# Two plain loads ahead of the transposing ones, setup fills on VectorE, eight sums as two, and new queue orders for every engine

## The chip, the cores and the metric

The kernel runs on one core of one Trainium2 chip. The metric is the device time of one execution in microseconds. TensorE (PE) multiplies, VectorE (DVE) and ScalarE (ACT) do everything between the products, GpSimd (POOL) does small copies and fills, and SyncE (SP) issues most of the transfers. ScalarE issues three small loads as well.

## The reference

`x` is 2 x 16000 x 512 in bf16. A depthwise filter of three taps along time and a SiLU give `z`. Four codebooks of eight vectors quantize it one after another, each on what the earlier ones left. The chosen vectors are summed and filtered by three more taps.

```python
for i in range(K):
    z = z + xp[:, i:i+T, :] * dw_enc[i][None, None, :]
z = _silu(z)
res = z
q = jnp.zeros_like(z)
for s in range(Nq):
    cb = codebooks[s]
    d2 = ...
    idx = d2.argmin(-1)
    sel = cb[idx]
    q = q + sel
    res = res - sel
...
for i in range(K):
    y = y + qp[:, i:i+T, :] * dw_dec[i][None, None, :]
```

## The kernel before

**Tiles.** Time is cut into 18 tiles of up to 16 x 128 = 2048 rows. Tiles 0 and 17 have 6 x 128 rows, tiles 1 and 16 have 8 x 128. Channels lie on the partitions, in four groups of 128 (`KT`), worked on in two halves.

**Loads.** Tiles 0 and 1 (`EARLY = 2`) come by one plain load each (`load_early`, L568) into `STAGE`, which is a part of the last `ZB` buffer, so the profile calls it `ZB`. TensorE transposes them (L579), and VectorE or ScalarE copies the result into `XT` (L589). From tile 2 on, `load` brings each group of 128 rows by a transposing load (L598, with L606 and L612 for the rows before and behind the tile).

**One tile's path.** `front` multiplies by the taps (L639 on ScalarE, L640 on VectorE) and adds (L391) into `ZB`; ScalarE takes an exponential (L645), one of the two adds 1 (L646, L647); `front2` takes a reciprocal (ScalarE, L657) and multiplies it into `ZB` (L391). The two functions of ScalarE need different tables, and each change is an `ACT_TABLE_LOAD`. `select` forms products with the codebooks (L676) and decides three of the four codebooks, one after another, in small VectorE steps. `rows` copies the one-hot rows to `OHR` (L791); `resid` subtracts the chosen vectors on TensorE (L834, L839) and copies the rest back into `ZB` (L861 on ScalarE, L862 on VectorE), decides the fourth codebook (L875 to L891) and copies the windows to `OHW` (L809). `back` forms the output on TensorE (L911 to L915), copies it to `YB` (L920, L921) and stores it (L948). Where TensorE would wait long, the program puts in filler products (L968), whose result is not used.

**Setup.** `setup` builds the constants: transposed codebooks `CBT` and `CBM2` (TensorE L420 and L430, ScalarE copies), the Gram matrix `GP` and its products `BD` (VectorE L391), the decoder rows `WDEC` (TensorE L551, VectorE L553), the selections `DJ`, `SEL`, `SEL3`, the 0/1 column sums `JM` (L496) and `SM` (L524), and fills. `make_identity` on GpSimd gives `IDENT`, which most of it reads. `WENC`, the taps (L397), needs `dw_enc` and the identity. Seven fills are GpSimd's (L381): `MSK`, two `OHD`, `ONES`, `CC2` and two `SEL3` (these lie in an `EX` buffer, so the profile calls them `EX`).

**Order.** The steps are listed by `add` with an engine, a cost and dependencies. The string `RANK` has two characters for each step, in the order of `add`; they are its place in the queue of its engine. The string `WHERE` has one letter for each step that may run on either of two engines (`either`): A for ScalarE, D for VectorE. So the two strings fix what each engine runs in which order; each engine takes its queue in order. The costs only decide which PSUM bank a step gets and where fillers go. There are 2410 steps, 608 of them movable.

Of the kernel before, what the change touches and what calls it, by code (L numbers as in the profile page):

```python
# [185 lines left out]
def kernel(  # L186
# [33 lines left out]
    RANK = ("000102000002060a0M0f0l150i0o0q020a080f0X0n0q0w0p0v0k0s0u0005040B0J010c030k0e0l0h0x090C0t0v0j0K0g0u01090c0f0i0k0n0p070d0e"  # L220
            "0h0j0m0o0q02040b04080a030506010307080d060e0b0g07090h0k0j0i0b090F0I0L0O0S0U130n0E0F0l0H0f0d0h0l10171c0Y1114080g0m0Z121607"
            "050c0s0o000m030n0p0E0G050P0Q0R0T0m0t0j0p040g0r060i0q0u0A0a0z0y0b0z1l1k0w0H020D0e0V0o1g0c0N0d0W1a190r181b1d1e1f0y1s0x1j1h"
            "1i1m1n1o1p0A1v0B1y0D1B0r0s1K1M1N1O1P1Q1R0r0t0L0u1T1V1X1Y1U1W1Z2021220s0v0O0w232426252728292a0t0x0R0y0z2e2f0A0B0T0U0C0D2k"
            "2i0E0F0X0Y0G0H2q2u2x2y2B0K120M150N160X0P1b101q1u1r1t1w0C1x1z0I0Q1A1C0G1D1E1G1F1H0K0M0d060g0c01050407080a0k0l030f0b0j0e09"
            "1L0J1J1I1S0N0P2b0S2l0V2r0W2o0Z2s0I0J2v2A2C2G2H2I2J0v0L140O2L2M2N2P2Q2S2V2W2X2Y0w0Q190R30323435363738390x0S3b0T0U3f1d0V0W"
            "3i1e0X0Y1h3k0Z103m1g11123o3q3u3v3x151m181p1b1u1n191r1a1x1m2h2d2g2c2j2n2m2p102D0r0B0z0i0y0v0w0u0q0t0s0x0n0p0A0o0h0m2w2t2z"
            "112F2K132O181a2R172U2T2Z31333a1c3h1f3n1j3t1l3H13143y16173A3B3D3F3G3I3J0y1c1q1e3L3N3O3S3P3U3V3X3Z410z1i451j434649484a4b4c"
            "4d0D1k1y1l1m1A4o1n1o1C1B1p1q1E1F1r1s1G4u1v1w4G1z1A4N4S4U4Y501J1Q1W231X261Z1Q1Z1T21201P1Y1Y25212127232a261d1f3T1g1h404244"
            "474e4g4i0A1t4w1u4l4n4t4y4x4z4A4B4C4D0B1x1I1y4E4F4H4J4K4L4M4O0C1C1L1D1F1P1R1H1K1T1S1L1M1V1W1N1O1X201U1V5x1Z205z5C5E5I5L27"
            "5R292c282e2s2a2d2b2f2a2r2r2w2t2q2y2v2p2w2k0N0J0P0F0E0D0O0G0R0H0L0M0I0K0T0Q0C0S3d3c3e3g3j1i3l3p1n3K1k3r3s3w3z1o3C3M1t4h15"  # L230
            "0Z1814131711160V1a0U0W1b121c1d190Y3Q3R3W1s3Y1v1w4f1z4q1D4v1H4I1K4X1B1E4V1G1I51535658595c2E5g0F1R5j1S5i5l5n5p5m5r5t5w5D5F"
            "0G2228255H5M5O5K5Q5S5U5W0J2c5Z2f2g2i2h2h2i2j2k2j2m2m2n2n2o2q2o2t2u6t2v2A6F6H6L6R6U2I6Y2T2L2W2N2Q2K2D2N2I2K2O2H2S2K2D2Q2J"
            "2V2T2O4p4m4k4j4r1J4s4P1N541l1i1q1u1v1x1j1k1f1t1p1s1g1e1w1r1h1o4T4Q1M4R4W1O4Z521U5e5a555b575d5h5f5k225y245G295X2b6524265T"
            "2d2e6364676a6d6f3E6h0I2q2p2s6j6l6n6p6k6o6q6r6s6u0L2x6w2z6v6x6y6z6A6B6C6D0P2B2x2D2F6T2A2G2H2B702J2L2E2G2Y312P2Q34357y3739"
            "7J7N7U7W7X3h313l363n38303j343v3d343k353p3a3c3t8c3q3c312k2l692C2E6M6O6P6S6V6X6Z0M2M2F2P7476777975787a7c7d7e0O2X7g2Z7i7j7m"
            "7l7p7q7r7s0Q337v36382W2U3b3d2Z2Y3e3f32303g3i33843o3s8d3u3w8j8m8o8u8A3H8G3Z3A423C3w3V3t3Y3z3A3P3q3U3u3x3N3r3Q3v3F1N1L1O1D"
            "1M1E1F1I1C1K1P1A1H1y1J1z1B1G5s5o5q5u5v5A5B5J2g6g5Y5N5V5P606162662l6m2725291T1U1X28231S1Q1V1Y1R22241W2c0E0H6e6b6c686i2s2u"
            "6E2y7b2z712C722O7x2R2U7f30327t7w7z7A7B7C7E0R3a2V3c7F7G7H7O7L7P7R7T7V7Z0S3m373r8185878e8g8i8l8n0T3x8q3y3z3i3f3A3D3h3j3F3I"
            "3l3o3J3K3p3n3R3T933W3X95979a9e9g433B4f3M4g3Q3H4k3P4p3S3M4i3T4r3W3P4s3V4u3X3W6K6J6I6G6N6Q6W732R7D2m2h2u2p2d2x2j2r2l2b2f2e"
            "2g2o2i2n0K0N2w7h2M7n7k7o7u2S7I2X7Y7M7K7Q7S80828386398p3b8r3e8t3g8I3B3C8w3E3G8C8F8E8H8J8L8M0U3O8Q3S8P8S8U8W8V8Y909194960V"  # L240
            "403x41989b9d9c9f9h9i9j0X449l46473E3F494a9v3J4b4c3H3I4d4e3K3L4h4j9M4n4o9R9T9Xa4a84zag4B414E43464A404C423V4F444G454b4R4f4S"
            "4j4m3L3M8O45489r9w9u9C9E9G9I0W4l3O4m9K9O9Q9U9P9S9Wa3a5a70Y4w3Y4yaaadafacahaiakam114Dao4H4I46474J4K49484L4M4a4b4P4QaM4d4T"
            "4VaT4X4Yb2b6babfbj5a4p5f4u5d4w4A5e4v5m4z4x5l4y5q4B4w5p4A5w4F4J2B2y2J2N2R2C2H2E2v2G2A2z2P2L2I2M2t2F888a898b8f8h8k8s3k8K8y"
            "8v8x8z8B3m8D8N3s992X3b372Y2T3639383d33353a2S2U322W2Z2V8T8X8Z8R923w3y9k3D9y3G9J3N9L3R9Y4q4ta24v4xabajaealaqatau0Z4NaE4Oaw"
            "ayaAaCaHaIaKaLaNaP104UaR4WaQaSaUaVaWaXaYaZ134Z4h5152b84l55564m4n58594o4q5b5c4r4s5g5hbv5k5nbFbJbQbTbV5F4N5J4R5R4U4L5N4S5V"
            "4W4S5S4V5W4X4N5X4Z61514R9n9p9o9m9q9s9t9x3Ua93t3v3h3k3u3i3p3g3q3o3r3l3e3f3m3n3s3j9B9A9z9D9F9H9N9V3Zapa19Za6a0anasarav4caO"
            "4eb04gb44ibq5053bc5457bdbgbiblbnbpbs125ibw5jbubxbBbEbzbCbGbIbKbM145t4D5ubObRbXbWbZc1c3c5155xca5y5z4Hcg5A5B4K4J5C5D4O4M5G"
            "5I4Pco5L5Mcw5P5QcDcIcKcMcO5Z5063536m5h526o5j6r5l4Z6f5g6n5i506e5f6pdK515o5sbS5r5vbYc0c2c4c6c7c8165E4L5Hc9cdcfckcncpcrcscu"
            "cx175Ocz5TcAcCcGcFcNcQcScU186252646555566667585768695a5b6b6d5cdo6g6idw6k6ldGdOdQdSdV6ze06I5w6T5I546P5C6S5G556H5x6M5D536E"
            "5s6G5v563S3G3E3K3B3N3J3z3D3T3R3Q3y3I3C3L3U3OazaDaxaBaFaJaGb14kbtb5b7b3b9bbbhbebk4xbP4e404f473Y483X4c493Z444a4g454143424d"  # L250
            "bm4tbobrbybAbDbH4Ecb4Gci4Icl4QcY5K5UcT5Y60cVcZcXd1d3d5d81a6adb6cdadcdgdidfdhdkdmdndp1b6hdt6jdrdsdudxdAdDdFdH1c6qdJ6t6vdW"
            "5m6w6y5oe16A6C5t5q6D6Fea5u6L6Oep6J6QevexezeBeC6WeJ7c5R7mfy5a7e5S7n5X577g5T7f5V597hfg7l5W584CbLbNbUcccechcj4TcR4o4n4q4i4u"
            "4s4v4r4l4C4t4k4h4y4p4j4B4zcmctcvcqcycBcEcH54d9cLcJcP4YcWd0d2d459dq5edI5kdT5ne76s6udN6x6Be2e5e4e8ebecee1e6K5z6Negeheielen"
            "eoeqeseteu1f6R5E6UeweyeAeDeEeFeGeH1h6XeI6Z70eQ5J72735LeR74765OeX77785Q5P7j7oft7r7wfEfIfSfTg27Ig97S6a7U6b5b7L667P675c7R69"
            "7Zgu5d836f856g5e6V6YeK7175eSeVeTeWeYf0f11g7af57df2f3f4f7fafbfcfdfeff1i7i5U7kfhfjflfkfmfnfofp1l7pfu7s7t5ZfD7v7x61fM7A7D62"
# [80 lines left out]
    JM = [sb([P, 1], F32, f"JM{j}") for j in range(4)]  # L336
# [7 lines left out]
    SM = [sb([P, 1], F32, f"SM{j}") for j in range(SL)]  # L344
# [48 lines left out]
    def setup():  # L393
# [3 lines left out]
        add("DVE", 0.15, ("setup", -7, 0), lambda: nc.vector.tensor_copy(WENC.rearrange("p k i -> p (k i)"), peb()), [], ["WENC"], free=box,  # L397
            after=[len(plan.steps) - 1])
# [12 lines left out]
        for b, t in enumerate(OHD):  # L411
            pool_memset(t, 0.0, [("OHD", b)], 0.6, ("setup", -4, 0))
# [593 lines left out]
```

## Time and profile before

| | us |
|---|---|
| median of 3 runs | 607.35 |
| the runs | 605.89, 607.7, 607.35 |
| profiled execution, its own time | 603.97 |
| its span | 602.2 |

The columns of the queue at the start, from the timeline of the profile: ScalarE's first compute comes at 5.89 us, its first exponential at 20.10, its first change of tables at 25.28. TensorE's granted clock was 0.978 of full speed over the span. The 26 table loads take 1.28 us each. ScalarE holds 114 output copies (L920) and VectorE 12 (L921).

How to read it: busy time is an average over stages with different limits. The page gives the busy time of each engine over the span, and a view by stretch gives the same for each stage. A row of the timeline has start, duration, engine, line, operation, output and input, the count, and in brackets the time that the engine sat idle before it, with what ended this.

### The profile page before, as it was taken

What the parts mean: (1) busy time and instruction counts of PE and PEld (TensorE: products, weight loads), DVE (VectorE), ACT (ScalarE), POOL (GpSimd) and SP (SyncE); (2) the same over time, 40 slices, a digit from 0 to 9 for tenths busy, and PEclk for the clock granted to TensorE, in tenths of its full rate; (3) what the DMA queues carried; (4) which work ended last, traced back from release to release, by engine and by line L of the source; (5) the groups of instructions that cost most, each with busy time, mean ns of one, the idle gap of its engine ahead of it and who ended that gap; (6) DMA issues with size and microseconds to landing.
All of it is one profiled execution on the core that took longest, in us unless ns stands there. A gap on an engine that the chain in (4) does not pass through costs nothing.

```text
span 602.2 us, 27782 instructions
## 1 busy us (share of the span) xinstructions
PE 500.1 (83%) x12621; PEld 240.2 (40%) x12621; DVE 564.9 (94%) x1117; ACT 546.2 (91%) x426; POOL 63.6 (11%) x93
## 2 busy tenths in 40 slices
PE   6979888588878886887787877888797889899995
PEld 3434334343434342343334243343434343445452
DVE  7999999999999999999999999999999999989774
ACT  5889799999999999999999999899999999994553
POOL 2010030000211020001011031101201120000000
PEclk9989999899998999999999988999998999999998
DMA  7534546454455856575875697576674624134146
GB/s 216 95 78 89 99 102 111 73 121 92 67 95 138 188 76 141 108 145 131 168 108 83 145 173 151 143 137 115 125 133 125 118 47 142 40 107 142 37 155 211
DMA packets 155564, 71.84 MB, mean 119 GB/s; under 512 B 146895, under 2 KB 146927, under 8 KB 155318
## 3 DMA queue, kind: packets, MB, share of 16 engines
q1 hardware_dynamic: 155230, 69.64, 53.9%
q8 instruction: 98, 1.61, 1.2%
q10 hardware_dynamic: 216, 0.43, 0.3%
q14 instruction: 20, 0.16, 0.1%
HBM read 2.26 MB, written 32.77 MB: 58 GB/s over the span
## 4 chain that ended last, share of the span: by engine, by line
DVE 35%; ACT 19%; PE 18%; SPq 14%; issue 9%; DMA 4%; POOL 0%; DVEq 0%; ACTq 0%
SPq L598 11%; DVE ZB L391 7%; DVE TA L391 5%; PE banks L834 5%; ACT EX L657 5%; DVE TB L640 5%; PE banks L839 4%; ACT ZB L861 4%; ACT EX L645 4%; DMA XT<-in_x_dram 3%; PE banks L676 3%; DVE TA L640 3%; PE banks L911 2%; ACT YB L920 2%; DVE EX L647 2%
## 5 line engine op out<-in xcount | busy, mean ns | idle before, releaser
L920 ACT CAST YB<-banks 128x1024 bf16<-128x1024 f32 x114 | 111.3, 1032 | 10.9 <-PE banks L911 4.8
L645 ACT ACTIVATE EX<-ZB 128x4096 bf16<-128x4096 bf16 (+2 forms) x36 | 115.5, 3208 | 4.5 <-DVE ZB L391 4.2
L657 ACT ACTIVATE EX<-EX 128x4096 bf16<-128x4096 bf16 (+2 forms) x36 | 115.2, 3202 | 0.1
L861 ACT CAST ZB<-banks 128x1024 bf16<-128x1024 f32 (+2 forms) x108 | 97.6, 955 | 16.0 <-PE banks L839 16.0
L968 PE MATMUL banks<-MSK,IDENT 128*128 128x512 bf16 x402 | 100.2, 390 | 8.2 <-issue 4.2
L676 PE MATMUL banks<-ZB 128*32 128x64 bf16 x8064 | 90.8, 198 | 11.1 <-issue 7.2
L676 PEld LDWEIGHTS <-ZB 128*32 128x32 bf16 x8064 | 76.3, 96 | 57.2 <-issue 50.1
L748 POOL COPY OHD<-OHA 128x256 bf16<-128x256 bf16 (+2 forms) x36 | 45.6, 1267 | 408.2 <-DVE OHA L391 377.6
L911 PE MATMUL banks<-WDEC,OHW 128*128 128x512 bf16 x252 | 74.6, 389 | 10.5 <-ACT YB L920 3.7
L839 PE MATMUL banks<-OHR,WR 32*128 32x512 bf16 (+2 forms) x1152 | 81.3, 353 | 0.6 <-issue 0.6
L640 DVE TENSOR_SCALAR TB<-XT,WENC 128x2048 bf16<-128x2048 bf16 (+2 forms) x119 | 80.2, 685 | 0.9 <-DVE EX L647 0.6
L391 DVE TENSOR_TENSOR TA<-TA,TB 128x4096 bf16<-128x4096 bf16 (+2 forms) x36 | 72.6, 2017 | 0.5
L391 DVE TENSOR_TENSOR ZB<-TA,TB 128x4096 bf16<-128x4096 bf16 (+2 forms) x36 | 72.6, 2018 | 0.4 <-ACT TB L639 0.2
L391 DVE TENSOR_TENSOR ZB<-ZB,EX 128x4096 bf16<-128x4096 bf16 (+2 forms) x36 | 72.4, 2015 | 0.4 <-ACT EX L657 0.4
L834 PE MATMUL banks<-ZB,IDENT 64*64 64x512 bf16 (+2 forms) x576 | 55.6, 365 | 14.3 <-ACT ZB L861 4.8
L968 PEld LDWEIGHTS <-IDENT 128*128 128x128 bf16 x402 | 37.9, 100 | 53.0 <-issue 16.7
L834 PE MATMUL banks<-ZB,UP 64*64 64x512 bf16 (+2 forms) x576 | 52.8, 350 | 0.0
L639 ACT ACTIVATE TB<-XT,WENC 128x2048 bf16<-128x2048 bf16 (+2 forms) x25 | 44.5, 1785 | 2.6 <-DVE TA L391 2.0
L839 PEld LDWEIGHTS <-WR 32*128 32x128 bf16 x1152 | 23.2, 92 | 58.7 <-issue 50.3
L640 DVE TENSOR_SCALAR TA<-XT,WENC 128x2048 bf16<-128x2048 bf16 (+2 forms) x64 | 43.2, 681 | 0.7 <-DMA XT<-in_x_dram 0.4
L834 PE MATMUL banks<-ZB,DOWN 64*64 64x512 bf16 (+2 forms) x576 | 41.2, 361 | 0.0
L862 DVE CAST ZB<-banks 128x1024 bf16<-128x1024 f32 (+2 forms) x36 | 34.4, 959 | 5.6 <-PE banks L839 5.4
(133 smaller groups left out, 580.8 us busy)
## 6 DMA issues: line engine op xcount, KB each, us to landing
out_dram<-YB SPq DMA_DIRECT2D x33, 448.0 KB
out_dram<-YB SPq DMA_DIRECT2D x28, 512.0 KB
XT<-in_x_dram SPq DMA_TRANSPOSE x267
out_dram<-YB SPq DMA_DIRECT2D x30, 60.0 KB
ZB<-in_x_dram SPq DMA_DIRECT2D x1, 1024.0 KB
ZB<-in_x_dram SPq DMA_DIRECT2D x1, 768.0 KB
out_dram<-YB SPq DMA_DIRECT2D x31, 2.0 KB
out_dram<-YB SPq DMA_DIRECT2D x2, 224.0 KB
```

What stands on the lines that cost most here:

```text
L391: add("DVE", cost, key, lambda: nc.vector.tensor_tensor(out=out, in0=a, in1=b, op=op), reads, writes, **kw)
L598: nc.sync.dma_start_transpose(out=X[:, :, g + 1, :], in_=src[g])
L640: lambda dst=dst, src=src, w=w: nc.vector.tensor_scalar(out=dst, in0=src, scalar1=w, scalar2=None, op0=ALU.mult),
L645: add("ACT", act(2 * R), ("exp", n, h), lambda: nc.scalar.activation(v(ex), Z, ACT.Exp, scale=-1.0), zt, [("EX", sl), "ACTTAB"], hold="E")
L657: nc.scalar.add_instruction(mybir.InstActivation(name=nc.get_next_instruction_name(), engine=mybir.EngineType.Activation, func=ACT.Reciprocal,
L676: nc.tensor.matmul(o[HB * q:HB * (q + 1), u * ZW:(u + 1) * ZW].rearrange("p (s c) -> p s c", s=2), lhsT=blk, rhs=both, start=False, stop=( ...
L834: nc.tensor.matmul(at(r)[to], lhsT=dia[h, h], rhs=Z[h, i, r:G:RG, :], start=start, stop=False)
L839: nc.tensor.matmul(at(r), lhsT=WR[v][g, i * P:(i + 1) * P], rhs=W[g, v // 3, 0:rows_of[r], :], start=False, stop=stop)
L861: either({"ACT": act_psum(2 * k * P), "DVE": dve(2 * k * P)}, key(1), lambda dst=dst, src=src: nc.scalar.copy(dst, src()), lambda dst=dst, ...
L911: nc.tensor.matmul(o, lhsT=W[:, k, PADC:PADC + P], rhs=WDEC[u], start=True, stop=not wrap)
L920: either({"ACT": act_psum(1024), "DVE": dve(1024)}, key, lambda dst=dst, box=box: nc.scalar.copy(dst, ps(box)), lambda dst=dst, box=box: n ...
L968: nc.tensor.matmul(PS[j // 2][:, 512 * (j % 2):512 * (j % 2) + NMK * ZW], lhsT=IDENT, rhs=MSK.rearrange("p u w -> p (u w)"), start=True, s ...
```

## The change

Five things are done:

1. The two plain loads of tiles 0 and 1 are the first two entries of SP's queue. The transposing loads of tile 2 list them as predecessors (`after=first_loads`). The planner's guess of how long a plain load takes changes.
2. Seven fills move from GpSimd to VectorE: `MSK` (128 x 512), two `OHD` (128 x 1024), `ONES` (128 x 128), `CC2` (24 columns of f32) and two `SEL3` (32 x 256); bf16 except `CC2`.
3. The four sums into `JM` become one into a tile `JMT` with four columns, and the four into `SM` one into `SMT`.
4. `RANK` and `WHERE` are new strings, for 2404 steps.
5. With them many movable steps change engine: of the taps with 2048 rows 8 go from VectorE to ScalarE and 4 back; of the output copies 8 and 7; of the corrections' copies with 1024 columns 10 and 9; of the copies to `OT` 4 and 12.

The heads of the queues, read off the strings:

| queue | before | after |
|---|---|---|
| SP | load 0, one transposing load, load 1, transposing loads | load 0, load 1, transposing loads |
| ACT | three loads, then codebook copies | two loads, one `CBM2` copy, the load of `WDBC`, codebook copies |
| PE | codebook, `ROW` product, Gram product, tile 0's first group, `WDEC` products, tile 1's first group, ... | codebook, tile 0's three groups, one group of tile 1, Gram product, ... |
| DVE | one `JM` sum, a fill, `DJ`, a fill, `SM`, `WENC`, ... | 17 fills, some copies and the two sums, `WENC` as the 25th, ... |

```diff
-        pool_memset(MSK, 0.0, ["MSK"], 0.8, ("setup", -6, 0))
+        dve_memset(MSK, 0.0, ["MSK"], 0.3, ("setup", -6, 0))
...
-            pool_memset(t, 0.0, [("OHD", b)], 0.6, ("setup", -4, 0))
+            dve_memset(t, 0.0, [("OHD", b)], 0.45, ("setup", -4, 0))
...
-        pool_memset(ONES, 1.0, ["ONES"], 0.3, ("setup", -5, 0))
+        dve_memset(ONES, 1.0, ["ONES"], 0.15, ("setup", -5, 0))
...
-        pool_memset(CC2, 0.0, ["CC2"], 0.2, ("setup", -5, 0))
+        dve_memset(CC2, 0.0, ["CC2"], 0.1, ("setup", -5, 0))
...
-        idv = IDENT.rearrange("p (s j c) -> p s j c", s=Nq, c=C)
-        for jj in range(4):
-            add("DVE", 0.2, key, lambda jj=jj: nc.vector.tensor_reduce(out=JM[jj], in_=idv[:, :, jj, :], axis=AX.XY, op=ALU.add), ["I"],
-                [("JM", jj)])
+        idv = IDENT.rearrange("p (s j c) -> p j s c", s=Nq, c=C)
+        add("DVE", 0.25, key, lambda: nc.vector.tensor_reduce(out=JMT, in_=idv, axis=AX.XY, op=ALU.add), ["I"], [("JM", jj) for jj in range(4)])
...
-            pool_memset(t, 0.0, [("SEL3", a), ("EX", NE - 1)], 0.4, ("setup", -5, 0))
+            dve_memset(t, 0.0, [("SEL3", a), ("EX", NE - 1)], 0.2, ("setup", -5, 0))
...
-        add("SP", 0.6, ("load", n, 0), lambda: nc.sync.dma_start(out=rows, in_=src), [], [("STAGE", n)], tail=2.0 + 0.35 * G)
+        first_loads.append(add("SP", 0.6, ("load", n, 0), lambda: nc.sync.dma_start(out=rows, in_=src), [], [("STAGE", n)], tail=2.4 + 0.3 * G))
...
-            add("SP", 1.4, ("load", n, 0.01 * g), lambda g=g: one(g), [], [("X", st["xb"], g + 1)], tail=1.5)
+            add("SP", 1.4, ("load", n, 0.01 * g), lambda g=g: one(g), [], [("X", st["xb"], g + 1)], tail=1.5, after=first_loads if n == EARLY else ())
```

The sums into `SM` change as those into `JM`.

More of the change, by code (lines that the diff above doesn't have):

```diff
@@ L343 @@
     WR = [sb([P, D], BF16, f"WR{v}") for v in range(4)]
-    SM = [sb([P, 1], F32, f"SM{j}") for j in range(SL)]
+    SMT = sb([P, SL], F32, "SMT")
+    SM = [SMT[:, j:j + 1] for j in range(SL)]
     MV = [sb([P, 1], F32, f"MV{v}") for v in range(3)]
@@ L605, in load @@
             before = xf[r0 - 1:r0 - 1 + G * P, :].rearrange("(p g) d -> g p d", g=G)[0]
-            add("SP", 1.4, ("load", n, 0.01 * G), lambda: nc.sync.dma_start_transpose(out=X[:, :, 0, :], in_=before), [], xe, tail=1.5)
+            add("SP", 1.4, ("load", n, 0.01 * G), lambda: nc.sync.dma_start_transpose(out=X[:, :, 0, :], in_=before), [], xe, tail=1.5, after=first_loads if n == EARLY else ())
         else:
```

105 lines of the change are left out of this document (53 added, 52 removed).

## The prediction

> **What bounds the kernel now.** I read the page first, then busy time by stretch, then VectorE's timeline where the last stretch begins.
>
> ```profile
> span 602.2 us, 27782 instructions
> ...
> PE 500.1 (83%) x12621; PEld 240.2 (40%) x12621; DVE 564.9 (94%) x1117; ACT 546.2 (91%) x426; POOL 63.6 (11%) x93
> ```
>
> Two engines are almost full, and TensorE's 83% contains fillers. Which engine is last depends on the stage. The columns below are the stretch, its length, and busy time with instruction counts of PE, PEld, DVE, ACT and POOL, then the granted clock and the DMA share.
>
> ```profile
> 0.00:46.00 46.00, 36.39 (x301) 18.00 (x301) 40.04 (x136) 35.84 (x52) 6.40 (x34) 0.96 0.54 129
> 46.00:523.60 477.60, 393.41 (x10326) 188.27 (x10330) 467.23 (x832) 463.26 (x322) 54.37 (x49) 0.98 0.59 117
> 523.60:590.00 66.40, 65.10 (x1894) 31.55 (x1884) 52.49 (x142) 43.26 (x50) 2.84 (x10) 1.00 0.32 111
> 590.00:602.20 12.20, 5.21 (x125) 2.42 (x124) 5.16 (x10) 3.87 (x4) 0.00 (x0) 0.87 0.63 202
> ```
>
> Up to 523.6 us VectorE is busy 507.3 us, so it idles 6.0 us in the head and 10.4 us in the body. From 523.6 to 590 TensorE is busy 65.1 of 66.4 us: that stretch is TensorE's, and the last 12.2 us are one chain. The border is this copy of tile 14's one-hot rows, with the wait before it in brackets:
>
> ```profile
> 522.78 0.29 DVE L391 TENSOR_TENSOR OHD<-KEY,M 128x128 bf16<-128x128 f32 x1
> 523.57 0.69 DVE L791 COPY OHR<-banks 128x1024 bf16<-128x1024 bf16 x1 [0.49 <-PE banks L786]
> ```
>
> TensorE's corrections of tile 14 (L841) wait for it. In the old and the new rank string TensorE has the same steps behind that point (100 of 533), and the final steps stand in the same order. So the time is the moment at which VectorE reaches this copy, plus 78.6 us that hardly shrink: TensorE idles 1.3 us before 590. The moment is VectorE's work ahead of the copy plus its idle time ahead of it. ScalarE is busy 499.1 us up to there and idles 24.5, so it is not the last.
>
> **The head now.** Start, duration, engine, line, tile, and the idle time before:
>
> ```profile
> 0.74 0.40 SPq L568 DMA_DIRECT2D ZB<-in_x_dram  x1
> ...
> 1.20 1.29 SPq L598 DMA_TRANSPOSE XT<-in_x_dram  x1
> ...
> 1.34 0.18 DVE L496 TENSOR_REDUCE JM<-IDENT 128x1 f32<-128x32 bf16 x1 [1.34 <-POOL IDENT masks.py:199]
> ...
> 1.80 0.43 ACTq L376 DMA_DIRECT2D YB<-in_dw_dec_dram  x1
> ...
> 2.55 0.56 SPq L568 DMA_DIRECT2D ZB<-in_x_dram  x1
> ...
> 4.11 0.17 DVE L397 CAST WENC<-banks 128x12 f32<-128x12 bf16 x1 [1.71 <-PE banks L396]
> ...
> 5.66 0.28 PE L420 MATMUL banks<-IDENT,CB 32*128 32x32 bf16 x4 [1.58 <-DMA CB<-in_codebooks_dram]
> ...
> 6.29 0.44 PE L430 MATMUL banks<-IDENT,CB 32*64 32x32 bf16 x6
> ...
> 6.88 1.03 PE L579 MATMUL banks<-IDENT,ZB 128*128 128x128 bf16 x8
> ...
> 10.36 1.04 PE L579 MATMUL banks<-IDENT,ZB 128*128 128x128 bf16 x8
> ...
> 13.98 0.69 DVE L589 COPY XT<-banks 128x1024 bf16<-128x1024 bf16 x1 [0.35 <-PE banks L579]
> ...
> 14.99 0.41 DVE L640 TENSOR_SCALAR TB<-XT,WENC 128x768 bf16<-128x768 bf16 x1
> ...
> 20.10 1.52 ACT L645 ACTIVATE EX<-ZB 128x1536 bf16<-128x1536 bf16 x1
> ...
> 28.09 0.96 DVE L391 TENSOR_TENSOR ZB<-ZB,EX 128x1536 bf16<-128x1536 bf16 x1
> ```
>
> VectorE starts at 1.34 us, when the identity is there, and waits another 1.71 us. Tile 0's transposes (L579) run from 6.88 us, between codebook work, and its taps start at 14.99 us.
>
> **The change, part by part.**
>
> **Plain loads first.** One transposing load is no longer between them, so the second is issued at about 1.2 us instead of 2.55. Its rows were used at 10.36 us and will be there about a transposing load (1.29 us) earlier, or more. The transposing loads of tile 2 move back by one plain issue, 0.4 us of a queue whose work is wanted only after the first two tiles; I take nothing. ScalarE's queue now issues the load of `WDBC` behind its first `CBM2` copy, which waits for the codebook: from 1.80 to about 6.1 us. TensorE wants it behind tile 0's and tile 1's transposes, near 11 us. It was used at the latest 6.2 us after issue (by 8.0), so TensorE could wait up to 1.3 us; its cover is the transposes, and I take nothing.
>
> **Memsets on VectorE.** Seven cross over. Rows for their price, and for the fused sums (tile and shape, count | busy, mean ns of one):
>
> ```profile
> L381 POOL MEMSET OHD<- 128x1024 bf16 x1 | 1.0, 1035 | 0.0
> ...
> L388 DVE MEMSET OHA<- 128x16 uint32 x8 | 0.5, 72 | 0.0
> ...
> L388 DVE MEMSET OHW<- 128x8 uint32 x6 | 0.4, 65 | 0.0
> ```
> ```profile
> L524 DVE TENSOR_REDUCE SM<-IDENT 128x1 f32<-128x32 bf16 x4 | 1.2, 288 | 0.0
> L496 DVE TENSOR_REDUCE JM<-IDENT 128x1 f32<-128x32 bf16 x4 | 0.7, 167 | 1.3 <-POOL IDENT masks.py:199 1.3
> ...
> L469 DVE TENSOR_REDUCE GD<-IDENT 128x16 f32<-128x128 bf16 x1 | 0.3, 254 | 0.0
> ```
>
> The two DVE rows give 7 ns for 8 more words: 0.9 ns a word on a base of 58 ns. A bf16 zero fill goes out as 32-bit words here (`OHA` is bf16 in the kernel), so 1024 elements are 512 words: 0.5 us for each `OHD`, 0.3 for `MSK`, 0.17 each for `ONES` and the two `SEL3`, 0.08 for `CC2`: 1.9 us. Without that packing it is twice the slope, about 3.4 us. I take 1.9, because both rows show packed words. The Trainium skill, page "VectorE: DVE Perf Modes", section "Zero memsets can be issued as uint32 (trn2)", says that a memset costs one cycle an element whatever the type, so only packing of zeros halves it; the trace's rows have that form, and by the page `ONES`, a fill with 1.0, stays unpacked, which these sums already have. The fills stand first in VectorE's new queue, before 4.11 us, where it idles 1.34 + 1.71 us now. If that cover went, 1.9 us would move the end.
>
> **Eight sums as two.** They take 1.2 + 0.7 us, or about 1.4 without overlap (neighbouring VectorE instructions overlap by some 0.07 us); the two new ones cost about 0.3 each by the L469 row. That is -0.8 us, with bounds of 0 and -1.4.
>
> **The head with all of it.** TensorE starts on the codebook at 5.66 us as now. Ten small transposes (0.28 + 0.44 us for ten) stand ahead of tile 0's three groups (about 1.0 each), so these end near 9.3, the copies near 10, and taps start at 10 instead of 14.99. VectorE's steps up to tile 0's first `ZB` add up to 5.2 us, so the first exponential comes at 15.3 instead of 20.10. But the products that used to fill the waiting (nine `BD`, four `WDEC`) now stand behind it, and the same addition puts the first gate product at 29.4, against 28.09. VectorE's idle time in the head falls from 6.0 to 3.8 us: 0.7 at the start, about 2 around tile 0's transposes, 1.1 in tile 0's decisions. That is **-2.2 us**. Its work ahead of tile 0's corrections grows by **2.4**: 0.8 in the setup (fills 1.9, less the fused sums and two `WR` products that change engines, less small reorderings), 1.3 for two `XT` copies taken from ScalarE, the rest in small ones.
>
> **All queues anew.** The strings fix each engine's order and the engine of every movable step, so I counted what VectorE has ahead of the copy at 523.57 in each, at these rows less the overlap:
>
> ```profile
> L640 DVE TENSOR_SCALAR TB<-XT,WENC 128x2048 bf16<-128x2048 bf16 x93 | 69.1, 751 | 0.8 <-DVE EX L647 0.6
> ...
> L862 DVE CAST ZB<-banks 128x1024 bf16<-128x1024 f32 x20 | 24.3, 1217 | 1.9 <-PE banks L839 1.9
> L921 DVE CAST YB<-banks 128x1024 bf16<-128x1024 f32 x12 | 14.5, 1219 | 2.7 <-PE banks L911 2.1 <-issue 0.4
> ...
> L758 DVE COPY OT<-banks 128x128 bf16<-128x128 bf16 x13 | 2.8, 217 | 0.4 <-PE banks L753 0.4
> ```
>
> Behind the head: four taps fewer (-2.7), taps of tiles 16 and 17 brought ahead (+2.0), two output casts (+2.3), six copies to `OT` (+0.9), one window copy (+0.6), corrections (-0.5): **+2.6 us**. ScalarE's own count changes by +0.7, and its table switches stay at 25. Whether the 2.6 cost anything depends on where they lie: in VectorE's 10.4 us of idle body they cost nothing, outside them 2.6.
>
> **Sum.** Head +2.4 - 2.2 = +0.2. Body: 2.6 us go into holes (0), and of the other 7.8 us of holes I take a third as closed, -2.6, between none and all, since the orders of all engines are new and no row shows the new waits. Together -2.4 us. On the profiled execution's 603.97 us (span 602.2) that is 601.6; the three runs lie at 605.89 to 607.7, all above it, and against their median of 607.35 it is **604.95**.
>
> **The rivals.**
>
> *Work brought ahead pushes the border (slower).* Place: VectorE ahead of the copy at 523.57. The added 2.6 us fall where it is already busy, and no hole closes: +0.2 + 2.6 = +2.8, so 610.15; with half of them in holes it is 608.85. It decides once VectorE idles more than 11.3 us before that copy (16.3 now, less the 5.0 us of added work). For it: VectorE is busy 467.2 of 477.6 us in the body, so little room is left. Against: a third of the holes is enough to hide the 2.6.
>
> *Most holes close (much faster).* Two thirds of the 7.8 us go: +0.2 - 5.2 = -5.0, so 602.35. For it: the order is what makes these waits. Against: tile 14's decisions wait on other engines in any order, as the 0.49 us at the copy shows.
>
> *The codebook lands behind the second plain load.* Up to 4.2 us, and from there to 5.05 (queue, packets, MB, share; q1 is SP's, q10 ScalarE's):
>
> ```profile
> q1 hardware_dynamic: 102, 0.63, 46.4%
> q10 hardware_dynamic: 24, 0.00, 0.4%
> ```
> ```profile
> q1 hardware_dynamic: 321, 0.23, 84.6%
> q10 hardware_dynamic: 51, 0.04, 20.7%
> ```
>
> The codebook's 0.03 MB, issued at 1.42, moved only when the first plain load's 0.79 MB were nearly through. Now 1.05 MB more stand right behind on SP's queue. If the codebook waits for these too, at the 322 GB/s of that stretch or the some 400 of a full one, it lands 2.5 to 3.2 us later, and TensorE holds tile 0's transposes behind it: -2.4 + 2.5 = +0.1, so 607.45. Against: ScalarE's queue got its turn when the load ahead of it was done. The Trainium skill, "DMA: Bandwidth & Descriptors", section "Queues, rings and completion order", has each DMA engine change between queues after a whole packet; by that rule the codebook comes between the two plain loads and lands as now, and the rows above agree so far.
>
> **How the numbers follow.** Forecast 0.50 (own range 603 to 607), border pushed 0.22, most holes close 0.14, codebook late 0.14. Less than 0.3% (1.8 us) cannot be told from no change here. Faster: 0.41 of the forecast, 0.14, and 0.04 of the late codebook, 0.59. Slower: 0.18 of the pushed border, 0.02 of the late codebook, 0.01 of the forecast, 0.21. Same: 0.20. The range 600.5 to 610.5 takes in the lower half of closing holes and the pushed border, and leaves out the case in which both the fills cost 3.4 us and no hole closes.
>
> **What would show it.** Right: L568 twice before any L598; VectorE's fills before 4 us with the 1.71 us gone; L640 from about 10 us; the first L645 near 15.3; the L391 gate near 29; L791 of tile 14 near 521 with VectorE's idle time ahead of it near 8.9 us; 78 us from there to the end. Wrong: L420 past 7 us (codebook late), fills longer than 0.8 us each, VectorE idle over 11 us ahead of that copy, or a stretch behind it that differs by more than 2 us, which would break the argument that it is TensorE's.

## The result and the profile after

| comparison | kernel before, median | changed kernel, median | ratio, 95% interval |
|---|---|---|---|
| first (12 and 12 runs) | 607.53 us | 603.06 us | 0.9934, 0.9910 to 0.9958 |
| second (29 and 12 runs) | 606.09 us | 603.55 us | 0.9948, 0.9927 to 0.9969 |

The change made the kernel faster by 0.5 to 0.7%; the medians lie 4.5 and 2.5 us apart, and 604.95 was forecast. Among the 29 runs of the kernel before in the second comparison, a granted clock lower by 0.01 goes with some 1.8 us more; the changed kernel's runs had 0.977 on average there and those 0.975, so by estimate some 0.4 us of the 2.5 may be the clock's. The two profiled executions of the prediction's pair lie only 1.5 us apart (span 602.2 and 600.7), because that of the kernel before was faster than all twelve unprofiled runs beside it (604.66 to 609.39). So a trace on each side isn't enough here, and both kernels were traced a second time.

The page of the changed kernel, its first lines:

```profile
span 600.7 us, 27780 instructions
...
PE 500.1 (83%) x12632; PEld 241.1 (40%) x12632; DVE 562.4 (94%) x1125; ACT 548.7 (91%) x419; POOL 53.6 (9%) x86
```

Busy time by stretch, cut at the new moment of tile 14's copy (columns as in the prediction: PE, PEld, DVE, ACT, POOL), and the copy itself:

```profile
0.00:46.00 46.00, 31.64 (x272) 16.19 (x273) 40.16 (x133) 33.74 (x50) 2.55 (x28) 0.93 0.56 131
46.00:523.23 477.23, 398.00 (x10367) 190.54 (x10369) 469.24 (x846) 465.85 (x316) 47.58 (x48) 0.99 0.60 116
523.23:590.00 66.77, 65.90 (x1983) 32.74 (x1976) 48.97 (x139) 44.32 (x51) 3.48 (x10) 1.00 0.37 127
590.00:600.70 10.70, 4.54 (x56) 1.67 (x40) 4.04 (x9) 4.80 (x5) 0.00 (x0) 0.87 0.54 175
```
```profile
523.23 0.68 DVE L792 COPY OHR<-banks 128x1024 bf16<-128x1024 bf16 x1
```

VectorE has 509.4 us of work ahead of the copy (507.2 before, up to that copy's start) and idles 13.8 us (16.3 before). TensorE is busy 65.9 of the 66.8 us behind it, as before, and the copy now waits for nothing. The head of the changed kernel, from its timeline:

```profile
0.74 0.91 SPq L569 DMA_DIRECT2D ZB<-in_x_dram  x2
...
0.86 0.27 DVE L390 MEMSET MSK<- 128x256 uint32 x1 [0.86 <-PEq L991]
1.19 0.48 DVE L390 MEMSET OHD<- 128x512 uint32 x1
...
1.81 0.17 DVE L390 MEMSET ONES<- 128x128 bf16 x1
...
7.00 0.23 PE L432 MATMUL banks<-IDENT,CB 32*64 32x32 bf16 x2 [3.44 <-DMA CB<-in_codebooks_dram]
...
9.00 0.69 DVE L590 COPY XT<-banks 128x1024 bf16<-128x1024 bf16 x1 [2.89 <-PE banks L580]
...
11.58 0.42 DVE L641 TENSOR_SCALAR TA<-XT,WENC 128x768 bf16<-128x768 bf16 x1
...
16.63 1.48 ACT L646 ACTIVATE EX<-ZB 128x1536 bf16<-128x1536 bf16 x1 [0.39 <-DVE ZB L393]
...
29.95 0.95 DVE L393 TENSOR_TENSOR ZB<-ZB,EX 128x1536 bf16<-128x1536 bf16 x1
```

The fills stand where they were expected, at the prices expected. But TensorE starts on the codebooks at 7.00 us instead of 5.66, and VectorE waits 2.89 us behind that. Three views of the DMA queues, up to 4.2 us, from there to 5.05 (q10 moves nothing) and from 5.05 to 6.3 us, show the codebooks' 0.03 MB on q10 in the last, which in the prediction's trace of the kernel before had moved by 5.05:

```profile
q1 hardware_dynamic: 121, 0.73, 45.0%
q10 hardware_dynamic: 24, 0.00, 0.4%
```
```profile
q1 hardware_dynamic: 56, 0.33, 93.1%
```
```profile
q1 hardware_dynamic: 64, 0.52, 100.1%
q10 hardware_dynamic: 42, 0.03, 7.9%
```

### The profile page after: what moved, and what is told of

Same layout as the page of the kernel before. It is cut to its first block, busy times and chain, and to the rows that moved or that the text cites. A ratio compares the mean times of both kernels' runs of the same rounds, so it can differ in the third digit from the quotient of the medians.

```text
span 600.7 us, 27780 instructions
## 1 busy us (share of the span) xinstructions
PE 500.1 (83%) x12632; PEld 241.1 (40%) x12632; DVE 562.4 (94%) x1125; ACT 548.7 (91%) x419; POOL 53.6 (9%) x86
## 4 chain that ended last, share of the span: by engine, by line
DVE 23%; PE 12%; SPq 8%; ACT 8%; issue 5%; DMA 1%; DVEq 0%; ACTq 0%
SPq L599 7%; DVE ZB L393 6%; DVE TB L641 3%; PE banks L835 3%; PE banks L912 3%; PE banks L677 2%; PE banks L840 2%; DVE TA L393 2%; ACT ZB L862 2%; DVE TA L641 2%; ACT EX L646 2%; DVE EX L648 1%; ACT YB L921 1%; DVE ZB L863 1%; DMA XT<-in_x_dram 1%
## 5 line engine op out<-in xcount | busy, mean ns | idle before, releaser
L862 ACT CAST ZB<-banks 128x1024 bf16<-128x1024 f32 (+2 forms) x109 | 97.7, 952 | 16.3 <-PE banks L840 16.3
L969 PE MATMUL banks<-MSK,IDENT 128*128 128x512 bf16 x413 | 103.5, 392 | 6.4 <-issue 2.6
L912 PE MATMUL banks<-WDEC,OHW 128*128 128x512 bf16 x252 | 74.0, 382 | 14.3 <-ACT ZB L862 8.0
L641 DVE TENSOR_SCALAR TB<-XT,WENC 128x2048 bf16<-128x2048 bf16 (+2 forms) x115 | 76.7, 676 | 1.6 <-issue 1.2
L835 PE MATMUL banks<-ZB,IDENT 64*64 64x512 bf16 (+2 forms) x576 | 54.3, 368 | 13.4 <-DVE ZB L863 3.0
L749 POOL COPY OHD<-OHA 128x256 bf16<-128x256 bf16 (+2 forms) x36 | 27.5, 764 | 417.3 <-DVE OHA L393 417.3
L969 PEld LDWEIGHTS <-IDENT 128*128 128x128 bf16 x413 | 38.4, 100 | 49.7 <-issue 13.8
L640 ACT ACTIVATE TB<-XT,WENC 128x2048 bf16<-128x2048 bf16 (+2 forms) x29 | 53.2, 1845 | 3.6 <-DVE TA L393 2.0
L863 DVE CAST ZB<-banks 128x1024 bf16<-128x1024 f32 (+2 forms) x35 | 32.8, 950 | 7.3 <-PE banks L840 7.3
```

The lines of the kernel that those rows point to most:

```text
L640: either({"ACT": act(R), "DVE": dve(R, 3.84) + 0.06}, key, lambda dst=dst, src=src, w=w: nc.scalar.mul(dst, src, w), lambda dst=dst, src=s ...
L641: lambda dst=dst, src=src, w=w: nc.vector.tensor_scalar(out=dst, in0=src, scalar1=w, scalar2=None, op0=ALU.mult),
L835: nc.tensor.matmul(at(r)[to], lhsT=dia[h, h], rhs=Z[h, i, r:G:RG, :], start=start, stop=False)
L862: either({"ACT": act_psum(2 * k * P), "DVE": dve(2 * k * P)}, key(1), lambda dst=dst, src=src: nc.scalar.copy(dst, src()), lambda dst=dst, ...
L912: nc.tensor.matmul(o, lhsT=W[:, k, PADC:PADC + P], rhs=WDEC[u], start=True, stop=not wrap)
L969: nc.tensor.matmul(PS[j // 2][:, 512 * (j % 2):512 * (j % 2) + NMK * ZW], lhsT=IDENT, rhs=MSK.rearrange("p u w -> p (u w)"), start=True, s ...
```

## The experiments

The moment of tile 14's copy, the rest behind it (span less moment), and VectorE's busy and idle time ahead of it were read the same way in every trace, from the copy's row and the view by stretch:

| profiled execution | its time | moment | rest | VectorE busy | idle |
|---|---|---|---|---|---|
| before | 603.97 | 523.57 | 78.6 | 507.2 | 16.3 |
| before, second trace | 608.32 | 528.45 | 78.0 | 507.9 | 20.6 |
| changed | 602.52 | 523.23 | 77.5 | 509.4 | 13.8 |
| changed, second trace | 603.50 | 524.01 | 77.7 | 509.4 | 14.6 |
| edits on the old order | 609.10 | 528.50 | 78.8 | 508.2 | 20.3 |
| the same, second trace | 608.74 | 528.17 | 78.7 | 507.7 | 20.5 |
| the same, fills on GpSimd | 607.59 | 527.65 | 78.2 | 507.1 | 20.5 |
| new order alone | 608.94 | 528.89 | 78.1 | 511.4 | 17.5 |
| the same, second trace | 606.57 | 525.75 | 79.1 | 511.1 | 14.7 |
| changed, fills on GpSimd | 602.22 | 522.75 | 77.6 | 510.4 | 12.4 |
| changed, codebooks first | 603.59 | 523.88 | 77.8 | 509.8 | 14.1 |
| changed, stores on GpSimd | 602.97 | 523.01 | 78.2 | 509.8 | 13.2 |
| changed, work added early | 611.10 | 531.51 | 77.8 | 515.0 | 16.6 |
| changed, work added late | 609.82 | 530.24 | 77.8 | 514.9 | 15.4 |

**Both kernels once more.** No edit.

> The kernel before, unchanged, for a second trace and as a null comparison. Expected: a ratio within 0.3% of 1. The first profiled execution took 603.97 us while twelve unprofiled ones took 604.66 to 609.39. If the end is set by the moment of VectorE's one-hot copy of tile 14 plus a tail of TensorE, a slower profiled execution must show the extra time as VectorE's idle time ahead of that copy (more than 16.3 us) or as a tail longer than 78.6 us, with busy times as before. If both stretches keep their length relative to the span, a lower clock made all instructions longer.

> The changed kernel, unchanged, for a second trace and a second comparison. Expected: 603 us and a ratio of 0.9934 within 0.25%. In its trace TensorE's tail behind tile 14's copy should be 77 to 79 us, as in the six traces so far, and whatever differs from the first trace should be VectorE's idle time ahead of the copy.

Before: 607.71 us, ratio 1.0014 (0.9994 to 1.0035). Changed: the second row of the first table. The slower execution of the kernel before has its 4.4 us as VectorE's idle time (20.6 against 16.3 us), with busy time and rest almost as before (0.6 us more and 0.7 less): the first possibility named. Some 3.0 us of the 4.3 are one wait, at a tap for a transposing load; the longest such wait in the first trace is 0.4 us. From the timeline of the second trace:

```profile
417.57 0.75 DVE L640 TENSOR_SCALAR TA<-XT,WENC 128x2048 bf16<-128x2048 bf16 x1 [3.41 <-DMA XT<-in_x_dram]
```

Against this execution the change is worth 4.4 us at the copy: 1.6 us more work and 6.0 us less idle time. Two stretches of the second traces show where, before and then changed (0 to 203 us, and 397 to 471):

```profile
0.00:203.00 203.00, 163.53 (x3131) 80.14 (x3132) 191.50 (x385) 183.56 (x144) 21.86 (x48) 0.97 0.54 107
...
397.00:471.00 74.00, 60.52 (x1803) 29.89 (x1802) 69.90 (x125) 69.42 (x48) 7.19 (x6) 0.95 0.63 122
```
```profile
0.00:203.00 203.00, 163.28 (x3246) 81.72 (x3280) 195.18 (x392) 188.07 (x143) 17.79 (x44) 0.97 0.54 108
...
397.00:471.00 74.00, 61.11 (x1746) 30.27 (x1752) 71.58 (x128) 70.43 (x52) 7.35 (x6) 0.98 0.62 118
```

In the first 203 us VectorE does 3.7 us more (195.18 against 191.50) in the same time, and ScalarE 4.5 more; from 397 to 471 us VectorE does 1.7 more, where the old order had its long wait. The other stretches up to 524 us differ by 0.3 us or less. The first traces don't repeat this: up to 203 us VectorE does only 0.4 us more there (192.80 against 192.37), and the rest of the difference is spread over the later stretches. So where the gain arises differs from execution to execution.

**The edits on the old order**, twice, and once with the fills left on GpSimd.

In short (the strings are left out):

```diff
 RANK, WHERE: those of before, but
-SP:  load 0, transposing load, load 1, ...
+SP:  load 0, load 1, transposing load, ...
-DVE: JM sum, fill, DJ, ... (eight sums); GpSimd: seven fills
+DVE: six fills, ... (two sums), one SEL3 fill once its place is free
```

> The three edits alone (both plain loads at the head of SP's queue, the seven fills on VectorE, eight mask sums as two) on the old order and the old choice of engines. Theory A, the gain comes from the new order of the body: the head's waits shrink by some 2 us, the fills cost as much, the time is 0 to 1.5 us below the kernel before (606 to 607.5). Theory B, the gain is in the head edits: at least 3 us below (604.5 or less). Theory C, the fills are paid in full: 1 to 2 us above.

> The three edits on the old order once more, for a second trace at an ordinary time, since the first profiled execution was one of the slowest of its kernel (609.1 against a median of 605.5). If the edits alone are worth 1.7 us, the ratio is again 0.995 to 0.999; its trace should then show VectorE past the head no later than in the kernel before and fewer or shorter waits for transposing loads. If the first ratio was chance, it is 1 within 0.3%.

> The old order with both plain loads at the head of SP's queue and two mask sums instead of eight; the seven fills stay on GpSimd. In the run with all three edits on the old order VectorE waited 3.0 us in the head for TensorE, which waited for the codebooks. Theory: the late codebooks cover the fills, so the fills cost nothing there, and this kernel takes what the three edits took together (605.5) within 0.3%, with tile 0's first gate at the same 29.1 us. Rival: the fills are paid, and this kernel is 1.9 us below it (603.6) with the gate near 27.3 us.

Ratios 0.9972 (0.9947 to 0.9996), 1.0024 (0.9999 to 1.0050) and, without the fills, 1.0015 (0.9992 to 1.0039). The first alone would have said 1.7 us faster; the repetition said the opposite. The two intervals just miss each other, so they are too narrow for comparisons made on different chips, and a single ratio nearer to 1 than about 0.3% is not to be read. Together they show no gain. Both traces with all three edits agree: 20.3 and 20.5 us idle, as in the second trace of before, and the first gate no earlier (29.15 and 29.23 us; 28.09 and 28.98 before). The head's waits of the first of them:

```profile
DVE GR L449 <- PE banks L445: 3.0, 1, 3.0
DVE rr L709 <- PE banks L675: 1.0, 1, 1.0
DVE MSK L390 <- PEq L989: 0.9, 1, 0.9
DVE WDEC L552 <- PE banks L550: 0.5, 1, 0.5
```

The 1.71 us of waiting for `WENC`'s product are gone (0.4 in the second trace), and 3.0 us (2.5) at the Gram matrix, which needs the codebooks, are new. With the fills on GpSimd the gate comes at 29.14 us, so the fills cost nothing here that shows, as expected: the wait for the codebooks covers them.

**The new order alone**, twice: the strings of the change, with the transposing load between the plain loads, the fills on GpSimd and eight sums.

In short again:

```diff
 RANK, WHERE: those of the change, but
-SP:  load 0, load 1, transposing load, ...
+SP:  load 0, transposing load, load 1, ...
-DVE: seven fills, two sums
+DVE: eight sums; GpSimd: seven fills
```

> The new order and the new choice of engines alone: one transposing load is between the two plain loads again, the seven fills are on GpSimd, eight mask sums instead of two. Theory A: most of the gain of the whole change stays, 2.5 to 4.5 us below the kernel before (603 to 605). Theory B: no gain (607.5 within 0.3%), since without the edits the new order has nothing to draw on. By the addition of VectorE's work, 2.6 us more stand ahead of tile 14's copy than before; if no wait closes, it is 2 to 3 us slower than before (609.5 to 610.5).

> The new order without the edits once more, for a second trace and comparison (the first profiled execution was the slowest of its kernel, 608.9 against a median of 605.3). If the order is worth 2 us alone, the ratio is again 0.995 to 0.9997. Its work on VectorE ahead of tile 14's copy is more than before; the gain must show as idle time of VectorE in the body, below the 10.4 to 14.3 us of the old order.

Ratios 0.9974 (0.9950 to 0.9997) and 0.9976 (0.9951 to 1.0001): about 1.5 us of the gain. Each ratio is too near to 1 to be read alone; that two chips agree speaks for it. It is less than theory A asked and more than theory B. What was expected of the second trace is not seen: VectorE's idle time in the body (from 46 us to the copy) is 13.5 and 11.5 us in these two traces, and not below the old order's range of 10.4 to 14.3. What is less is the head's, 3.9 and 3.2 us against 6.0 and 6.3. Both profiled executions were slower than the median of their twelve, by 3.7 and 2.4 us. Here the first codebook product starts at 5.59 us in both traces, against 6.91 to 7.07 in the nine with both plain loads ahead and the codebooks on ScalarE's queue: the late codebooks come from the loads. The head is none the worse for the missing edits (first gate at 29.42 and 28.54 us; 29.95 with them), so what the whole change has beyond the order isn't in the head. One place shows in the traces: from the copy of tile 12's one-hot rows to that of tile 13's it takes 29.87 and 29.60 us here, and 28.0 us in all seven other traces on the new order. First the second trace of the new order alone, then the second trace of the changed kernel:

```profile
468.91 0.60 PE L968 MATMUL banks<-MSK,IDENT 128*128 128x512 bf16 x2
...
470.58 0.82 PE L968 MATMUL banks<-MSK,IDENT 128*128 128x512 bf16 x3 [1.06 <-issue]
471.24 0.38 PE L911 MATMUL banks<-WDEC,OHW 128*128 128x512 bf16 x1
...
472.13 1.01 ACT L920 CAST YB<-banks 128x1024 bf16<-128x1024 f32 x1 [1.47 <-issue]
...
480.99 0.23 DVE L758 COPY OT<-banks 128x128 bf16<-128x128 bf16 x1 [1.19 <-PE banks L753]
```
```profile
469.05 0.82 PE L912 MATMUL banks<-WDEC,OHW 128*128 128x512 bf16 x2 [0.27 <-DVE OHW L810]
...
470.34 1.03 ACT L921 CAST YB<-banks 128x1024 bf16<-128x1024 f32 x1
470.36 0.81 PE L969 MATMUL banks<-MSK,IDENT 128*128 128x512 bf16 x3 [0.49 <-issue]
...
479.54 0.21 DVE L759 COPY OT<-banks 128x128 bf16<-128x128 bf16 x1
```

The order of the steps is the same. But five fillers stand ahead of tile 11's output products in the first and three behind them in the second: the planner places fillers by the steps' costs, and undoing the edits changes these. TensorE comes to the products 2.2 us later, ScalarE waits 1.47 us for its cast, its casts of the rest come late, TensorE's corrections wait for those, and VectorE waits 1.19 us for a transpose queued behind them. Between 430 us and tile 14's copy this trace loses 1.5 us on the changed kernel's second trace and 1.3 on its first, nearly all of it at this place. The medians on one chip put what the edits add in all at 1.1 us (604.14 against 603.06 with the fills on GpSimd, below) and at 1.9 us (605.27 against 603.42 with the codebooks first). So probably most of it is a side effect of their costs. The run with the codebooks first has the PSUM banks of the new order alone in tile 12's corrections and no such wait, so it isn't the banks; no run moves the fillers alone, so this cause is argued from the rows and not shown by a run.

**The changed kernel with its fills back on GpSimd** (4 of the planner's 433 bank choices differ, none behind the setup).

```diff
-        dve_memset(MSK, 0.0, ["MSK"], 0.3, ("setup", -6, 0))
+        pool_memset(MSK, 0.0, ["MSK"], 0.8, ("setup", -6, 0))
...
```

> The changed kernel with the seven fills back on GpSimd; loads first, two sums and the new order stay. Extra work on VectorE behind the head went to the end in full (7.55 us of fills made the kernel 7.0 and 7.9 us slower). Theory: in the head the wait for the codebooks covers the fills, so tile 0's first gate stays at 29.9 us and the time at that of the changed kernel, 603.3 within 0.3%. Rival: the fills are in VectorE's way in the head too, the gate comes 1 to 2 us earlier and the time falls as much. Third: GpSimd is late with them, and it is slower.

603.06 us, ratio 0.9964 (0.9935 to 0.9993, which takes in the changed kernel's two ratios); the first gate at 29.89 us. The theory holds as far as this can tell: where the fills run makes no difference that shows. The rows of the head show something else, told in the last section.

**The codebooks first.**

```diff
-    jw = add("ACT", 0.6, ("setup", -9, 0), lambda: nc.scalar.dma_start(out=CB1, ...), writes=["CB1"], tail=2.2, after=[jw])
+    jw = add("SP", 0.4, ("setup", -9, 0), lambda: nc.sync.dma_start(out=CB1, ...), writes=["CB1"], tail=2.2)
```

> The changed kernel with one move: the load of the codebooks goes from ScalarE's queue to the head of SP's queue, ahead of both plain loads. In the changed kernel TensorE waits for it until 7.00 us and VectorE idles 2.89 us behind that. If VectorE's idle time in the head goes straight to the border (theory A of the prediction: moment of the copy is work plus idle), the time is 1.5 to 2.5 us below the changed kernel, 600.5 to 601.5. Rival: a later wait in the body takes up what the head gives back, and the time stays at that of the changed kernel, 603 within 0.3%. If the plain loads come later by as much, tile 0's first transposes wait for these instead and the gain is under 1 us.

603.42 us in six runs, ratio 0.9931 (0.9906 to 0.9956): the changed kernel's time. The head did gain: first codebook product at 2.95 us, first gate at 27.74 instead of 29.95. Theory A misses: tile 14's copy comes at 523.88 us, between the changed kernel's 523.23 and 524.01, so none of the 2.2 us shows at the border. The rival says that later waits take them, and these are VectorE's longest at taps:

```profile
114.69 0.75 DVE L641 TENSOR_SCALAR TA<-XT,WENC 128x2048 bf16<-128x2048 bf16 x1 [0.95 <-DMA XT<-in_x_dram]
...
179.38 0.75 DVE L641 TENSOR_SCALAR TB<-XT,WENC 128x2048 bf16<-128x2048 bf16 x1 [1.35 <-issue]
...
213.72 0.75 DVE L641 TENSOR_SCALAR TA<-XT,WENC 128x2048 bf16<-128x2048 bf16 x1 [1.44 <-issue]
```

The first is a wait for a transposing load; the two with "issue" have no releaser in the profile, but stand at the same kind of step. VectorE's steps have the same order in these kernels, so the same taps can be compared. In the changed kernel's second trace they start at 115.33, 179.15 and 211.97 us, with no wait over 0.5 us: the lead of 2.2 us is gone at the second. In its first trace they start at 116.99, 181.56 and 214.37 us:

```profile
116.99 0.75 DVE L641 TENSOR_SCALAR TA<-XT,WENC 128x2048 bf16<-128x2048 bf16 x1 [1.35 <-DMA XT<-in_x_dram]
...
181.56 0.75 DVE L641 TENSOR_SCALAR TB<-XT,WENC 128x2048 bf16<-128x2048 bf16 x1 [1.23 <-issue]
```

It waits at the first two itself, and the lead lasts until the third. So the rival holds, but which wait takes the lead differs between two executions of one kernel. SP's loads came no earlier than in the second trace, and 2.0 us earlier than in the first (where the first load below is issued at 168.62 us). Here is SP's queue with the codebooks first and then in the changed kernel's second trace:

```profile
166.59 1.26 SPq L613 DMA_TRANSPOSE XT<-in_x_dram  x1
167.90 1.26 SPq L607 DMA_TRANSPOSE XT<-in_x_dram  x1
```
```profile
166.54 1.27 SPq L613 DMA_TRANSPOSE XT<-in_x_dram  x1
167.85 1.27 SPq L607 DMA_TRANSPOSE XT<-in_x_dram  x1
```

**Work added**, early (behind the gate at 65 us) and late (at about 500 us).

```diff
+    SCR = sb([P, 496], BF16, "SCR")
+    for j in range(20):
+        add("DVE", 0.0, ("extra", 0, j), lambda: nc.vector.memset(SCR, 0.0), [], [])
```

> The changed kernel with 20 extra fills of a scratch tile (248 words each, about 0.27 us by the rows of the fills, 5 us together) on VectorE right behind the gate at 65 us; nothing reads the tile. If VectorE's work ahead of tile 14's copy goes to the end whatever its place (theory A, the border), the time is 5 us above the changed kernel: 608. Rival, which the codebook run points to: waits for transposing loads between 110 and 350 us take up part of it, as they took the 2.2 us given in the head, and it is 1.5 to 3.5 us above (604.5 to 606.5).

> The same 20 extra fills, 5 us, on VectorE at about 500 us, some 25 us ahead of tile 14's copy. Theory A: 5 us above the changed kernel, 608, with the tail behind the copy at 77 to 79 us as before. Rival: TensorE and not VectorE sets the stretch behind 500 us; its fillers shrink, the tail gets shorter by some of the 5 us, and the time is under 2 us above the changed kernel.

The group's row, the same in both kernels (count | busy us, mean ns | idle time before them):

```profile
L974 DVE MEMSET SCR<- 128x248 uint32 x20 | 5.3, 265 | 2.2
```

So a block takes 7.5 us, not 5: the fills all write one tile, and there is a gap of 0.11 us on average between each two that the expectation left out. The times are 610.51 and 611.44 us, 7.0 and 7.9 above the changed kernel's 603.55 on the same chip (the late one in six runs); in the traces the copy comes 7.5 and 6.2 us later. About all of it reaches the end, from either place, and the rest behind the copy stays at 77.8 us. Theory A holds for work that is added, and both rivals fall.

**The stores off SP's queue.**

```diff
-            nc.sync.dma_start(out=view[p0:p1, lo:hi, :], in_=Y[p0:p1, lo - g0:hi - g0, :])
+            (nc.gpsimd if st["n"] <= 10 else nc.sync).dma_start(out=view[p0:p1, lo:hi, :], in_=Y[p0:p1, lo - g0:hi - g0, :])
```

> The changed kernel with the output stores of tiles 0 to 10 issued from GpSimd's queue instead of SP's, everything else in its place. In the traces so far VectorE's longest waits in the body (1.0 to 3.4 us) are taps that wait for a transposing load, and SP issues these loads one behind the other with stores between them. Theory: the stores hold the loads up; then these waits of 1 to 3 us go and the time is 1 to 3 us below the changed kernel (600 to 602). Rivals: the loads come late for another reason (their buffer comes free late), and the time stays at 603 within 0.3%; or GpSimd, which carries steps of the decisions, is held by the stores' waits for their casts, VectorE then waits for GpSimd, and it is over 2 us slower than the changed kernel.

606.77 us, ratio 1.0007 (0.9976 to 1.0038), runs from 602.97 to 611.14: 3.2 us above the changed kernel on the same chip. The profiled execution was the fastest of its twelve, and even there VectorE waits 3.4 us for transposing loads:

```profile
DVE TB L641 <- DMA XT<-in_x_dram: 3.4, 2, 2.6
```
```profile
L949 POOL DMA_DIRECT2D out_dram<-YB x80 | 48.0, 605 | 86.6 <-ACT YB L921 84.9 <-DVE KEY L393 1.1 <-issue 0.2
```

The longer of the two waits ends at 342.84 us, after a stretch in which SP issued transposing loads and nothing else (319.13 to 340.53 us). So taking the stores away doesn't end these waits, and GpSimd pays 48 us for issuing them. What costs its other runs up to 8 us more is not shown, since the profile is of the fastest. None of the kernels tried is clearly faster than the changed one.

## Why the prediction was right, and where it was not

**The border: right for most of the gain.** In fourteen traces the rest behind tile 14's copy is 77.5 to 79.1 us, while the copy moves between 522.75 and 531.51, and the added fills show by force that work ahead of it goes to the end. One pair of traces doesn't measure the gain. In the prediction's pair the copy comes only 0.3 us earlier, and the rest is 1.2 us shorter; between the second traces it is 4.4 and 0.3. Taking the five traces on the old order against the five of the changed kernel and its variants without added work, the copy comes 3.9 us earlier on average, and the rest is 0.7 us shorter; the prediction took next to nothing for the rest.

**The balance of work against idle time: right in kind, with both terms too large.** The forecast was 5.0 us more work and 7.4 less idle time, so a copy 2.4 us earlier. Measured: in the prediction's pair 2.2 us more work and 2.5 less idle time, between the second traces 1.6 more and 6.0 less. Both terms are smaller than forecast, and these errors work against each other in the sum. That 604.95 comes within 2 us of the measured medians is in part luck. Most of the listed items came as counted; two of them in rows of the changed kernel beside those of the prediction:

```profile
L641 DVE TENSOR_SCALAR TB<-XT,WENC 128x2048 bf16<-128x2048 bf16 x88 | 65.1, 747 | 1.5 <-issue 1.2
...
L759 DVE COPY OT<-banks 128x128 bf16<-128x128 bf16 x17 | 3.6, 213 | 0.1
...
L542 DVE TENSOR_SCALAR DJ<-IDENT,JMT 128x128 bf16<-128x128 bf16 x4 | 0.9, 234 | 0.0
```

What the sum lacked: one copy of one-hot rows fewer ahead of the border (-0.7 us), and VectorE's other setup steps, which get shorter when GpSimd stops filling. The four `DJ` take 234 ns each here, and before:

```profile
L543 DVE TENSOR_SCALAR DJ<-IDENT,JM 128x128 bf16<-128x128 bf16 x4 | 1.6, 393 | 0.0
```

The run with the fills back on GpSimd shows the size: VectorE has 510.4 us of work there instead of 509.4, though by the rows it has 1.8 us of fills less.

**The fills: right.** 0.27, 0.48 and 0.17 us where 0.3, 0.5 and 0.17 were worked out, and covered, as the run without them shows. `ONES` went out unpacked and the zeros packed. The Trainium skill, "VectorE: DVE Perf Modes", section "Zero memsets can be issued as uint32 (trn2)", says this of zeros; the rows agree.

**The step that failed: "TensorE starts on the codebook at 5.66 us as now".** It starts at 7.00, the mark set for "wrong" (and at 6.47 in the second trace of the kernel before, so "now" is itself not one number). With that the head's -2.2 us of idle time did not come (head idle time 6.0 before, 5.8 after; 6.3 and 5.3 in the second traces). In the new order alone, where the codebooks are used at 5.59 us, it did: 3.9 and 3.2 us. In the changed kernel the taps started at 11.58 instead of 10 and the first exponential at 16.63 instead of 15.3. So the rival of the late codebooks had its mechanism, at half its size or less (1.34 us and 0.52 between the second traces, instead of 2.5). The prediction's sentence on the Trainium skill's "DMA: Bandwidth & Descriptors", section "Queues, rings and completion order", by which the codebooks should land as before between the two plain loads, does not agree with the trace: their packets moved only from 5.05 us on, when 1.06 MB of SP's queue had gone (0.73 by 4.2 us and 0.33 more by 5.05). Why they stood so long no run shows. The rival's price was wrong too, the other way: a head that is 2.2 us earlier gained nothing that shows at the end, so the late codebooks cost the forecast nothing there.

**The holes: met in one pair only.** The forecast has the body's idle time fall by 5.2 us (2.6 filled with work, 2.6 closed). It fell by 2.4 in the prediction's pair (10.4 to 8.0) and by 5.0 between the second traces (14.3 to 9.3). Between the second traces it lies mostly in the first 203 us, where work was brought forward into idle time; the first traces do not show this.

**"Border pushed" fell, though its sign was there.** The prediction named over 11 us of idle time ahead of the copy as a sign of being wrong, and it is 13.8 and 14.6 us. The sign took 5.0 us of added work for granted. With the work measured, the same sum breaks even at 14.1 us in the prediction's pair (16.3 less 2.2) and at 19.0 between the second traces (20.6 less 1.6): the added work did go into holes, in the first pair only just.

**Not foreseen: the fillers.** The prediction went through the order, the engines and the edits, and not through the costs that the edits change; these moved fillers, and this cost, by the traces, some 1.3 to 1.5 us between the new order alone and the whole change.

**The base.** The sum was made on one profiled execution of the kernel before, 3.4 us under the median, and then carried to the median. That worked for the number, not for the holes: the 10.4 us of idle body are that execution's, the second has 14.3, and what an order can close is counted from that.

## What to carry to other kernels

Where one engine is nearly full up to a fixed border, work added to it goes to the end in full, but time given to it early may be taken back by a later wait; ask for each saved microsecond what the engine will then wait for. Take a second trace of the kernel before you size its waits, and repeat a comparison on another chip before you read a third of a per cent. Where a planner goes by costs, an edit that changes them can move work far away from it.

## What the runs showed of the hardware

**GpSimd's fills slow VectorE.** The same VectorE step on 128 x 128 numbers takes 0.17 us in the changed kernel and 2.10 us beside GpSimd's fills. First the changed kernel with its fills on GpSimd, then the changed kernel:

```profile
2.50 2.10 DVE L533 TENSOR_SCALAR DOWN<-IDENT 128x128 bf16<-128x128 bf16 x1
...
2.86 1.03 POOL L383 MEMSET OHD<- 128x1024 bf16 x1
```
```profile
3.13 0.17 DVE L533 TENSOR_SCALAR DOWN<-IDENT 128x128 bf16<-128x128 bf16 x1
```

The Trainium skill, "SBUF — State Buffer", section "SBUF: two separate sides", says that VectorE in its two-port modes and GpSimd share a port pair that one of them holds for a whole instruction while the other waits. These rows agree with it, though no run shows the ports, and the step waits longer than any one fill takes. Here the wait was hidden behind the codebooks; in a head without that cover, fills on VectorE might be the cheaper ones; no run shows that.

**A queue behind another.** 0.03 MB on ScalarE's queue wait for 1 MB on SP's queue when the plain loads stand together, and less when a transposing load stands between them (first codebook product at 7.00 against 5.59 us, on the same order of ScalarE's queue; 5.66 and 6.47 in the two traces of the kernel before).

**Transposing loads jitter.** The longest wait for one is 3.41 us in one trace of the kernel before and 0.4 in the other; 3.0 of the 4.3 us between these two executions are that wait, and the runs of the first comparison spread over as much (604.66 to 609.39 us).
